# One-level Strassen in both products of the first token pair, with the weight factors made elsewhere

## The chip, the core and the metric

The kernel runs on one core of a Trainium2 chip. That core has five engines with a queue each: TensorE (PE, matrix products; PEld is its weight load), VectorE (DVE), ScalarE (ACT), GpSimd (POOL) and SyncE (SP), which here only issues DMAs. An engine works through its own queue in order, and a semaphore holds it until what an instruction needs is there. The metric is the device time of one launch in microseconds; lower is better. Three runs of the kernel before took 1492.28, 1492.61 and 1493.27 us.

## What is computed

```python
scores = scale * (q_chunk @ k_chunk^T)                 # 8 x 8 heads, 576 tokens in chunks of 64, head size 64
attn   = softmax(scores)
x      = (attn @ v) as [4608 tokens, 512]
p      = domain_probs / sum(domain_probs)              # [4608, 4]
for e in range(4):                                     # w1: [4, 512, 1024], w2: [4, 1024, 512]
    h    = maximum(x @ w1[e], 0)
    out += p[:, e] * (h @ w2[e])
```

Everything is float32. A float32 operand goes to PE as two halves, a high part (a cast to the reduced type `F32R`) and a low part (what is left), and each product is three matmuls: high x high, high x low, low x high.

## The kernel before

**Tiles and stages.** The 4608 tokens are nine sub-blocks of 512. The first one goes alone; the other eight go as four pairs. The 1024 hidden columns of an expert are two halves of 512, so that each sub-block or pair sees eight passes (4 experts x 2 halves); pass n is pass n % 8 of its stage. A pass multiplies x by a 512 x 512 piece of w1, takes the positive part h, and multiplies h by a 512 x 512 piece of w2.

- *First sub-block* (n = 0 in `startup`, n = 1 to 7 in `plain_pass`): both products plain. Four steps for the hidden columns (`plain_hidden`), then four output tiles of 128 tokens (`Tile.whole`), 12 matmuls of 128 x 512 each: 96 in a pass. The attention of pair 0 runs beside them (`Beside`, a generator that is given one step at a time).
- *First pair* (n = 8 to 15, `first_pair_pass`): x w1 by one-level Strassen (`Group`: seven products of 2 x 3 matmuls, in two groups of 128 columns: 84 matmuls), h w2 plain on eight token tiles (96 matmuls). 180 in a pass.
- *Later pairs* (n = 16 to 39): both products by Strassen, 84 + 84 = 168 matmuls in a pass. `first_later_pass` (n = 16) does x w1 alone; each `later_pass` weaves x w1 of its own pass (`g`, `h` steps) with h w2 of the pass before (`a`, `b` steps) in the order `WOVEN`, 28 steps of 6 matmuls; `last_products` does the last h w2 alone.

**Strassen's sums.** The token side needs sums and differences of h (or x) quarters: `Scaled` and `Tokens`. Of each, ACT casts the high part (`hi`) and POOL subtracts it for the low part (`lo`). Names: b11, b22, b12, b21 are quarters, t1 to t4 the sums; each has two halves k. The weight side needs 7 factors per weight and column group: a11, a12, a22 and s1 to s4. `Factors` makes them in the first pair (sums on POOL, casts on ACT, low parts on POOL) and writes them to DRAM in 7 slots per pass and weight; from n = 16 on `ring_load` reads them back, 512 KB a slot, into a ring of three tiles per weight (`wf0` to `wf5`). `ring_next` asks for the slot three further on as soon as a slot's two units are used (`Units.done`).

**What sets the order.** All orders are written out by hand (`tc.manual_schedule()`): a step's matmuls are issued, then the functions listed for that step (`at`), engine by engine in program order. `TILES` says in which pass and step the attention tiles of the next pair come. PE's PSUM results are read by ACT (`keep`) and DVE.

**Lines.** L513 is every product, L326 and L329 the casts and low parts of weights and tokens, L368 the weight sums, L692 and L695 high and low parts of h, L686 sums of h, L680 relu with scaling, L521 relu's low part in the plain product, L814 the plain output, L463 sums of x, L315 the weight loads, L404 and L408 the writes of factors, L418 the ring's loads.

## Time and profile before

| what | value |
|---|---|
| runs | 1492.28, 1492.61, 1493.27 us (median 1492.61) |
| profiled execution, span from first to last instruction | 1490.5 us |
| PE busy | 1482.5 us (99%) |
| DVE, ACT, POOL busy | 945.3, 611.9, 870.6 us (63, 41, 58%) |
| first sub-block, about 0 to 203.5 us | POOL busy 90.7 of the first 203.0 us |
| first pair, about 203.5 to 545.6 us | PE busy 342.10 of 342.10 us, POOL 231.62 |
| later pairs, 545.6 us to the end | POOL busy about 22 of each 38 to 40 us |

The page gives no end-to-end time for the profiled execution beside its span; the median of the runs lies 2.1 us above the span. How to read it: a row "start, length, engine, line, operation, out<-in, xN" merges N instructions in a row of one kind, and a bracket at its end tells how long the engine stood idle before it and who released it. PE's matmuls overlap: a 128 x 512 matmul is listed with 389 ns, but 24 of them in a row take 5.44 us.

### The profile page before, as it was taken

The page shows a single profiled execution, that of the slowest core. Times are in us where ns is not written, and L with a number is a line of the kernel's source. Part 1 is how long each engine was busy: PE and PEld are TensorE (multiplying, and loading weights), DVE is VectorE, ACT ScalarE, POOL GpSimd, SP SyncE. Part 2 cuts the span into 40 slices and gives each one's busy share as a digit, 9 for nine tenths or more (in the row PEclk, how much of TensorE's full clock was granted, in tenths as well). Part 3 has the DMA queues.
Part 4 walks back from the last instruction along what each step waited for, and adds up shares of the span by engine and source line. Part 5 has one row for each costly group of instructions (what it writes and reads, how often), then busy time and mean ns, then how long its engine had stood idle before and what let it go on. Part 6 is the DMA issues. An engine that isn't in the chain of part 4 may idle for free.

```text
span 1490.5 us, 23245 instructions
## 1 busy us (share of the span) xinstructions
PE 1482.5 (99%) x8652; PEld 1219.7 (82%) x8652; DVE 945.3 (63%) x1338; ACT 611.9 (41%) x1143; POOL 870.6 (58%) x666
## 2 busy tenths in 40 slices
PE   8999999999999999999999999999999999999998
PEld 7888888888888888888888888888888888888887
DVE  5454654544444466777776977777778866666666
ACT  3454454444544434434343434343433433333232
POOL 2353587677757616555566755555557655555554
PEclk9999999999999999999999999999999999999999
DMA  6454348977767576767766679667666696666665
GB/s 200 128 158 126 116 156 305 313 244 228 247 228 240 200 265 212 235 196 235 217 213 195 217 209 277 210 217 229 211 196 197 207 244 213 192 206 190 207 196 155
DMA packets 211088, 314.16 MB, mean 211 GB/s; under 512 B 54800, under 2 KB 131360, under 8 KB 210976
## 3 DMA queue, kind: packets, MB, share of 16 engines
q1 hardware_dynamic: 210976, 312.69, 66.5%
q8 instruction: 68, 1.11, 0.3%
q14 instruction: 44, 0.36, 0.1%
HBM read 244.39 MB, written 68.23 MB: 210 GB/s over the span
## 4 chain that ended last, share of the span: by engine, by line
PE 99%; DVE 0%; ACT 0%; issue 0%; ACTq 0%
PE A L513 49%; PE C L513 30%; PE B L513 17%; PE psa L208 1%; PE psa L161 1%; PE B L912 0%; PE C L962 0%; PE A L892 0%; PE B L898 0%; DVE psa L233 0%; DVE e L240 0%; ACT xh L326 0%; PE A L912 0%; PE psa L892 0%; PE C L1433 0%
## 5 line engine op out<-in xcount | busy, mean ns | idle before, releaser
L695 POOL TENSOR_TENSOR hfl<-wraw,hfh 128x512 fp32r<-128x512 f32 x288 | 374.3, 1316 | 215.6 <-ACT hfh L692 213.6
L513 PE MATMUL A<-xh,wf 128*128 128x512 f32 (+1 forms) x1104 | 378.4, 388 | 0.0
L513 PE MATMUL A<-hfh,wf 128*128 128x512 f32 (+1 forms) x768 | 268.4, 391 | 0.0
L692 ACT CAST hfh<-wraw 128x512 fp32r<-128x512 f32 x288 | 176.0, 622 | 214.4 <-DVE wraw L686 63.6
L575 ACT COPY s<-A 128x512 f32<-128x512 f32 x192 | 112.5, 587 | 321.2 <-PE A L513 320.5
L513 PEld LDWEIGHTS A<-xh,wf 128*128 128x128 f32 x1104 | 206.8, 188 | 42.9
L513 PE MATMUL A<-xl,wf 128*128 128x512 f32 (+1 forms) x552 | 213.7, 388 | 0.0
L513 PE MATMUL C<-xh,wf 128*128 128x512 f32 (+1 forms) x600 | 203.3, 388 | 0.7 <-ACT xh L326 0.7
L513 PEld LDWEIGHTS A<-hfh,wf 128*128 128x128 f32 x768 | 144.1, 188 | 31.5 <-DVE acc L742 1.2
L742 DVE TENSOR_TENSOR acc<-A,acc 128x512 f32<-128x512 f32 x174 | 118.7, 683 | 63.3 <-PE A L513 62.7
L513 PE MATMUL A<-hfl,wf 128*128 128x512 f32 x384 | 149.2, 389 | 0.0
L513 PE MATMUL C<-hfh,wf 128*128 128x512 f32 x384 | 133.6, 389 | 0.0
L513 PEld LDWEIGHTS C<-xh,wf 128*128 128x128 f32 x600 | 111.4, 188 | 23.9 <-ACT xh L326 0.8
L329 POOL TENSOR_TENSOR hfl<-wraw,hfh 128x512 fp32r<-128x512 f32 x64 | 85.9, 1371 | 77.0 <-ACT hfh L326 68.9
L513 PE MATMUL B<-xh,wf 128*128 128x512 f32 (+1 forms) x376 | 124.7, 383 | 0.0
L329 POOL TENSOR_TENSOR wf<-wraw,wf 128x512 fp32r<-128x512 f32 x70 | 91.5, 1331 | 55.0 <-ACT wf L326 49.6
L513 PEld LDWEIGHTS A<-xl,wf 128*128 128x128 f32 x552 | 103.5, 188 | 21.1
L513 PE MATMUL C<-xl,wf 128*128 128x512 f32 (+1 forms) x300 | 114.6, 385 | 0.0
L686 POOL TENSOR_TENSOR wf<-wraw,wf 128x512 f32<-128x512 f32 x23 | 29.7, 1292 | 139.3 <-DVE wf L680 139.3
L742 DVE TENSOR_TENSOR acc<-C,acc 128x512 f32<-128x512 f32 x90 | 62.1, 690 | 44.7 <-PE C L513 37.5
L695 POOL TENSOR_TENSOR hfl<-wf,hfh 128x512 fp32r<-128x512 f32 x48 | 70.1, 1461 | 32.4 <-ACT hfh L692 31.9
L513 PEld LDWEIGHTS C<-hfh,wf 128*128 128x128 f32 x384 | 72.1, 188 | 14.9
(185 smaller groups left out, 2747.8 us busy)
## 6 DMA issues: line engine op xcount, KB each, us to landing
wf<-w SPq DMA_DIRECT2D x336, 512.0 KB, 4.1
wraw<-in_w SPq DMA_DIRECT2D x128, 256.0 KB, 3.9
w<-wf SPq DMA_DIRECT2D x112, 256.0 KB, 4.6
qk_in<-in_qk SPq DMA_DIRECT2D x32, 512.0 KB, 4.8
w<-hfl SPq DMA_DIRECT2D x32, 256.0 KB, 3.8
w<-hfh SPq DMA_DIRECT2D x32, 256.0 KB, 3.3
w<-hfh SPq DMA_DIRECT2D x48, 128.0 KB, 2.9
w<-hfl SPq DMA_DIRECT2D x48, 128.0 KB, 2.8
```

The lines of the kernel that those rows point to most:

```text
L161: nc.tensor.matmul(s["sc"][of_half(half), c, slot], lhsT=q, rhs=k, start=True, stop=True)
L208: nc.tensor.matmul(av[of_half(slot % 2), half, head // 2], lhsT=s["v"][of_half(half), head], rhs=s["pt"][of_half(half), c, slot], start=Tr ...
L329: eng.tensor_tensor(out=t[1], in0=src, in1=t[0].bitcast(F32), op=ALU.subtract)
L513: nc.tensor.matmul(out, lhsT=lhs(k, a), rhs=rhs(k, b), start=first and i == 0, stop=last and i == len(parts) - 1, skip_group_check=not (fi ...
L575: nc.scalar.copy(out=t, in_=self.a)
L686: (eng or nc.vector).tensor_tensor(out=self.values[place, k], in0=self.values[a, k], in1=self.values[b, k], op=op)
L692: nc.scalar.copy(out=self.part(name, 0)[:, k], in_=self.values[name, k])
L695: (eng or nc.gpsimd).tensor_tensor(out=self.part(name, 1)[:, k], in0=self.values[name, k], in1=self.part(name, 0)[:, k].bitcast(F32), op=A ...
L742: nc.vector.tensor_tensor(out=acc[key], in0=src, in1=acc[key], op=ALU.add)
```

## The change

1. **First pair.** `first_pair_pass` is gone. The pair runs through `first_later_pass` (now n = 8) and `later_pass` (n = 9 to 39), so h w2 is done by Strassen there too: 168 matmuls a pass for 180.
2. **w2's factors** are made in the first sub-block: sums on DVE (on POOL in pass 0), casts on ACT, low parts on POOL, then 20 writes a pass to the slots (`keep_quad`, `keep`).
3. **w1's factors** for passes 0 to 6 are made in the first pair itself, a column group ("half") at a time: `half_load` fetches it, four sums of 128 x 256 on POOL, and each ring slot, in place of a load, is two casts on ACT and two low parts on POOL of 128 x 256 (`ring_make`, one slot per step at most through `make_next`), and a write for the later pairs. Those of pass 7 are made in passes 2 to 5 (`LAST_W1`, `keep_unit`).
4. **Places.** The x of pair 1 no longer stays in SBUF: each attention tile is written to DRAM (`x_kept`) and read back in pass 15 (`x_back`), as `xraw` now holds the halves. In the first sub-block w1's raw quarters go to accumulator tiles (`acc4` to `acc7`).

```diff
@@ a_copy
+        if pair == 1:
+            tile_x = scratch[0][:, :SUB].rearrange("p (j q) -> p j q", j=NK)
...
+        if pair == 1:
+            nc.sync.dma_start(out=x_kept[:, :, i * P : (i + 1) * P], in_=tile_x)
...
+    def x_back():
+        xraw[1] = xpool.tile([P, NK, PAIR * SUB], F32, name="xraw")
+        for k in range(NK):
+            nc.sync.dma_start(out=xraw[1][:, k], in_=x_kept[:, k])
@@ half factors
+    class HalfFactors:
+        AT = {"a11": 0, "a12": 1, "a21": 2, "a22": 3, "s1": 4, "s2": 5, "s4": 6, "s3": 2}
...
+        def less(self, name, a, b, eng, op=ALU.subtract):
+            (eng or nc.gpsimd).tensor_tensor(
+                out=self.at[name], in0=self.at[a], in1=self.at[b], op=op
+            )
...
+    def ring_make(r):
+        t, (n, k) = ring[0, r], divmod(r, N_SLOT)
+        for u in range(2):
+            g, at = divmod(2 * k + u, 7)
+            src = halves[n_pass + n, g].at[ORDER[0][at]]
+            nc.scalar.copy(out=t[:, u, 0], in_=src)
+            nc.gpsimd.tensor_tensor(out=t[:, u, 1], in0=src, in1=t[:, u, 0].bitcast(F32), op=ALU.subtract)
+        nc.sync.dma_start(out=slots[n, 0, k], in_=t.bitcast(F32))
+
+    def make_next():
+        if making:
+            making.pop(0)()
...
+        if i == 0 and r < n_made:
+            making.append(begin)
+        else:
+            begin()
@@ plain_pass
+        w2 = []
+        add(at, 1, lambda: w2.append(w2_factors(n)), lambda: w2[0].sum1(nc.vector), lambda: w2[0].sum2(nc.vector))
+        add(at, 2, lambda: w2[0].sum3(nc.vector), lambda: w2[0].sum4(nc.vector))
+        for i, quad in enumerate(KEPT):
+            add(at, 2 + i // 2, lambda quad=quad: keep_quad(n, *quad))
+        for i, name in enumerate(("s1", "s2", "s3", "s4")):
+            add(at, (3, 4, 5, 5)[i], lambda name=name: w2[0].make(name))
+            add(at, (4, 5, 6, 6)[i], lambda name=name: w2[0].keep(name))
...
-            add(at, 5, lambda: w_loads(1, n + 1))
+            add(at, 6, lambda: w_loads(1, n + 1, PAIR_QUADS))
...
+        add(at, 0, lambda: half_load(n + 1, 0))
+        add(at, 2, lambda: halves[n + 1, 0].sum1(), lambda: halves[n + 1, 0].sum2())
+        add(at, 3, lambda: halves[n + 1, 0].sum3(), lambda: halves[n + 1, 0].sum4())
+        for r in range(6):
+            add(at, (2, 4, 5, 6, 6, 6)[r], lambda r=r: ring_load(0, r, (RINGS[0] + RINGS[1])[r]))
+            if r < 3:
+                add(at, (2, 4, 5)[r], make_next)
+        add(at, 5, lambda: half_load(n + 1, 1))
+        add(at, 6, *(lambda s=s: getattr(halves[n + 1, 1], s)() for s in ("sum1", "sum2", "sum3", "sum4")))
...
-    def first_pair_pass(n, held, made, beside):
...
@@ first_later_pass
+        add(at, 0, lambda: half_load(n + 1, 0))
+        add(at, 5, lambda: half_load(n + 1, 1))
+        half_sums(at, n + 1, 0, (5, 5, 6, 6))
+        half_sums(at, n + 1, 1, (10, 10, 11, 11))
@@ later_pass
+        if n + 1 < 2 * n_pass - 1:
+            add(at, 5, lambda: half_load(n + 1, 0))
+            add(at, 17, lambda: half_load(n + 1, 1))
+            half_sums(at, n + 1, 0, (9, 10, 11, 13))
+            half_sums(at, n + 1, 1, (23, 25, 26, 27))
+        if n == 2 * n_pass - 1:
+            add(at, 0, x_back)
...
+            make_next()
@@ the main sequence
-        for n in range(n_pass, 2 * n_pass):
-            held, made = first_pair_pass(n, held, made, beside[1])
-        ahead = (None,) * 3
-        for n in range(2 * n_pass, n_run):
-            ahead = (later_pass if n > 2 * n_pass else first_later_pass)(n, *ahead)
+        ahead = first_later_pass(n_pass, held)
+        for n in range(n_pass + 1, n_run):
+            ahead = later_pass(n, *ahead)
```

**Place 1: POOL in the first pass of the woven stage.** Before, this is n = 16: `hfl0` to `hfl5` are low parts of h (hfl0 is b11, hfl2 b22, hfl1 b21, hfl5 t2, hfl4 t1), up to the second half of b21.

```order
L695 TENSOR_TENSOR hfl0_5667<-wraw_5655,hfh0_5665 128x512
L695 TENSOR_TENSOR hfl2_5701<-wraw_5688,hfh2_5699 128x512
L695 TENSOR_TENSOR hfl0_5667<-wraw_5711,hfh0_5665 128x512
L695 TENSOR_TENSOR hfl1_5750<-wraw_5734,hfh1_5748 128x512
L695 TENSOR_TENSOR hfl5_5761<-wraw_5655,hfh5_5759 128x512
L695 TENSOR_TENSOR hfl4_5780<-wraw_5688,hfh4_5778 128x512
L695 TENSOR_TENSOR hfl2_5701<-wraw_5776,hfh2_5699 128x512
L695 TENSOR_TENSOR hfl1_5750<-wraw_5797,hfh1_5748 128x512
```

Now it is n = 8, and the same queue from the fifth ring slot of pass 8 (`wf5`) on reads as follows; `wf` are ring slots being made (two instructions each), `xraw` the half sums.

```order
L489 TENSOR_TENSOR wf5_2724<-xraw_2633,wf5_2724 128x256 x2
L489 TENSOR_TENSOR wf0_2737<-xraw_2633,wf0_2737 128x256 x2
L489 TENSOR_TENSOR wf1_2755<-xraw_2633,wf1_2755 128x256 x2
L786 TENSOR_TENSOR hfl2_2772<-wraw_2753,hfh2_2770 128x512
L444 TENSOR_TENSOR xraw_2633<-xraw_2633 128x256 x4
L786 TENSOR_TENSOR hfl0_2722<-wraw_2786,hfh0_2720 128x512
L489 TENSOR_TENSOR wf4_2813<-xraw_2633,wf4_2813 128x256 x2
L786 TENSOR_TENSOR hfl1_2831<-wraw_2809,hfh1_2829 128x512
L786 TENSOR_TENSOR hfl5_2842<-wraw_2689,hfh5_2840 128x512
```

The eight low parts of h stand in the same order, but ring slots and half sums of the next pass now stand between them.

**Place 2: SP at the end of the first sub-block** (pass 7). Before, where the ring is filled for the first time (end of the first pair), six loads stand in a row:

```order
L418 DMA wf0_5506<-w0_0_0_96 128x1024
L418 DMA wf1_5508<-w0_0_1_97 128x1024
L418 DMA wf4_5510<-w0_0_2_98 128x1024
L418 DMA wf3_5512<-w0_0_3_99 128x1024
L418 DMA wf2_5514<-w0_0_4_100 128x1024
L418 DMA wf5_5516<-w0_0_5_101 128x1024
```

Now the first three slots are made and written (L490), and the load of the second half, `xraw<-in_w1`, stands behind the write of the third, which waits for POOL's low part of that slot:

```order
L490 DMA w0_0_1_98<-wf1_2598 128x1024
L909 DMA out_0<-acc1_521 128x512
L411 DMA w7_1_1_203<-hfl6_2593 128x512
L411 DMA w7_1_4_206<-hfl6_2593 128x512
L490 DMA w0_0_2_99<-wf4_2627 128x1024
L439 DMA xraw_2633<-in_w1 128x4x128 x2
```

**Place 3: DVE in pass 6**, between the low part of the first hidden block (hfl0) and that of the last (the second hfl1). Before:

```order
L521 SCALAR_TENSOR_TENSOR hfl0_1981<-A1_2011,hfh0_1980 128x512
L463 TENSOR_TENSOR xraw_891<-xraw_891 128x2x512
L521 SCALAR_TENSOR_TENSOR hfl1_2039<-B0_2040,hfh1_2038 128x512
L329 TENSOR_TENSOR xl4_2036<-qk_in_2009,xh4_2035 128x1024
L521 SCALAR_TENSOR_TENSOR hfl1_2039<-B1_2059,hfh1_2038 128x512
```

Now, with the four sums of w2 (L389) in the same stretch:

```order
L615 SCALAR_TENSOR_TENSOR hfl0_2233<-A1_2263,hfh0_2232 128x512
L389 TENSOR_TENSOR ws_2286<-wraw_2198,wraw_2194 128x512
L389 TENSOR_TENSOR ws_2286<-ws_2286,wraw_2192 128x512
L557 TENSOR_TENSOR xraw_954<-xraw_954 128x2x512
L615 SCALAR_TENSOR_TENSOR hfl1_2294<-B0_2295,hfh1_2293 128x512
L389 TENSOR_TENSOR wraw_2198<-wraw_2192,wraw_2198 128x512
L389 TENSOR_TENSOR wraw_2196<-wraw_2196,ws_2286 128x512
L346 TENSOR_TENSOR xl4_2291<-qk_in_2261,xh4_2290 128x1024
L615 SCALAR_TENSOR_TENSOR hfl1_2294<-B1_2324,hfh1_2293 128x512
```

Two sums stand ahead of the third block's low part and all four ahead of the fourth's.

More of the change, by code (lines that the diff above doesn't have):

```diff
@@ L310, in w_load @@
     def w_load(i, n, f, k):
-        t = raw[i, f, k] = wpool.tile([P, 2, 2 * P], F32, name="wraw", bufs=N_RAW)
+        if i == 0 and n:
+            t = opool.tile([P, 2, 2 * P], F32, name=f"acc{NK + 2 * f + k}")
+        else:
+            t = wpool.tile([P, 2, 2 * P], F32, name="wraw", bufs=N_RAW)
+        raw[i, f, k] = t
         e, half = divmod(n % n_pass, 2)
```

338 lines of the change are left out of this document (175 added, 163 removed).

## The prediction

> **What bounds the kernel now.** I read the page's busy times and its chain first, then the chain in order of time for the pitch of the matmuls, then busy time by stretches.
>
> ```profile
> span 1490.5 us, 23245 instructions
> ...
> PE 1482.5 (99%) x8652; PEld 1219.7 (82%) x8652; DVE 945.3 (63%) x1338; ACT 611.9 (41%) x1143; POOL 870.6 (58%) x666
> ...
> PE 99%; DVE 0%; ACT 0%; issue 0%; ACTq 0%
> ```
>
> PE is the bound in nearly every moment. The rows below, of the chain in order of time, show how regular it is.
>
> ```profile
> 92.22 5.44 PE A L513 x24
> ...
> 1286.85 4.11 PE A L513 x18
> ...
> 1324.95 4.08 PE A L513 x18
> ...
> 1363.03 4.08 PE A L513 x18
> ```
>
> 24 matmuls in 5.44 us are 0.2267 us each, 6 are a step of 1.36 us. The same point of a pass returns after 1363.03 - 1324.95 = 38.08 us, which is 168 x 0.2267: a later pass without attention has no gap at all. So PE's work is what I save from, and every wait that the change brings to PE is added in full.
>
> ```profile
> 203.50:545.60 342.10, 342.10 (x1971) 281.60 (x1970) 164.93 (x247) 158.45 (x300) 231.62 (x181) 1.00 0.76 256
> 545.60:567.40 21.80, 21.80 (x98) 18.06 (x97) 12.23 (x18) 8.67 (x15) 10.55 (x8) 1.00 0.50 162
> 1324.95:1363.03 38.08, 38.08 (x170) 31.54 (x169) 24.80 (x33) 11.72 (x20) 22.06 (x18) 1.00 0.63 194
> ```
>
> Each row is a stretch: length, then busy time of PE, PEld, DVE, ACT and POOL, clock, DMA. The granted clock is 1.00 throughout. In the first pair (first row) POOL is busy for 231.62 of 342.10 us; in a later pass for 22.06 of 38.08 us.
>
> **What is saved.** In the first pair h w2 goes from 96 to 84 matmuls in each of 8 passes: 96 fewer, all of 128 x 512 on PE's path. 96 x 0.2267 = 21.8 us. Nothing else that PE does there changes in number. DVE, ACT and DMA get the same evacuations and ring traffic as a later pass, which runs without a gap; I cost them at nothing. The same holds for reading x of pair 1 back in pass 15 (up to one or two us if late).
>
> **What POOL gets in the first pair.** The added instructions are 128 x 256, a shape that POOL does not have in this trace, so I bound it by its neighbours.
>
> ```profile
> L368 POOL TENSOR_TENSOR ws<-wraw x16: 1282/1290/1312, 197.7 to 495.9; 128x512 f32<-128x512 f32 x16
> ...
> L463 POOL TENSOR_TENSOR xraw<-xraw x2: 2398/2414/2431, 819.2 to 1135.9; 128x1024 f32<-128x1024 f32 x2
> ...
> L219 ACT COPY xraw<-psa x32: 364/372/374, 59.5 to 1100.0; 128x256 f32<-128x256 f32 x32
> ```
>
> 512 more columns cost 2.41 - 1.29 = 1.12 us, so 256 columns cost 1.29 - 0.56 = 0.73 us; half of 1.29, 0.645, is the lower bound, and 1.29 the upper. I take 0.73. ACT's share of a slot, two casts of about 0.37 us, hides in its idle time (11.72 of 38.08 us busy).
>
> *Term 1, the way from pass 7 into pass 9.* In the pass that begins the woven stage now, POOL has to bring b21's last low part for step a2. Before:
>
> ```profile
> 550.93 1.29 POOL L695 TENSOR_TENSOR hfl<-wraw,hfh 128x512 fp32r<-128x512 f32 x1 [8.84 <-ACT hfh L692]
> ...
> 564.82 2.60 POOL L695 TENSOR_TENSOR hfl<-wraw,hfh 128x512 fp32r<-128x512 f32 x2 [0.26 <-ACT hfh L692]
> ...
> 567.39 2.72 PE B L513 x12
> ```
>
> The last of eight low parts ends at 567.42, a2 starts at 567.39 and needs it with its fifth matmul, 0.91 us on. 0.88 us of room, with 10.55 us of work in 21.8. Now the same stretch on PE is 21.8 + 2.72 us (the output tile held over from pass 7) + 0.91 = 25.4 us. POOL's queue holds eight low parts, 10.55 us, six ring slots, 12 x 0.73 = 8.8, and twelve half sums, 12 x 0.73 = 8.8: 28.1 us, 2.7 more than the stretch has even from a standing start. And it does not start standing. POOL in pass 7:
>
> ```profile
> 185.72 5.44 PE B L513 x24
> ...
> 194.25 3.54 POOL L329 TENSOR_TENSOR hfl<-wraw,hfh 128x512 fp32r<-128x512 f32 x2 [1.01 <-ACT hfh L326]
> ...
> wraw<-in_w SPq DMA_DIRECT2D x128, 256.0 KB, 3.9
> qk_in<-in_qk SPq DMA_DIRECT2D x32, 512.0 KB, 4.8
> ```
>
> w2's low parts end at 197.79, 12.1 us after the pass's first matmul. Then come four half sums and three slots, 10 x 0.73 = 7.3 us, and four low parts of w2's sums, 4 x 1.29 = 5.2: 24.6 us. The load of the second half is queued on SP behind the third slot's write; two loads of the kind above take about 5 us with their issue, so POOL goes on at 29.6 us and is through with the 28.1 us at 57.7. PE's need is at 19.04 (seven steps of 2.72 in pass 7) + 25.4 = 44.4 us. **PE waits 13.3 us**, in pieces at the first h step (slot 3), at a1 and at a2. Bounds: with 0.645 for a small one, w2's low parts at 1.29 each (done at 9.2) and a load of 3.9 us it is 5 us; with POOL's instructions stretched by a tenth and 7 us for the load, 18.
>
> *Term 2, five boundaries between passes 9 and 14.* Each of these passes has 14 low parts for the ring and 8 half sums, 22 x 0.73 = 16.1 us, on top of 22.06: 38.2 us of POOL in a pass of 38.08 plus about 1.2 per attention tile. Before, around a boundary:
>
> ```profile
> 1308.55 3.80 POOL L695 TENSOR_TENSOR hfl<-wraw,hfh 128x512 fp32r<-128x512 f32 x3 [0.16 <-ACT hfh L692]
> 1312.81 1.29 POOL L695 TENSOR_TENSOR hfl<-wraw,hfh 128x512 fp32r<-128x512 f32 x1 [0.47 <-ACT hfh L692]
> ...
> 1316.71 1.29 POOL L695 TENSOR_TENSOR hfl<-wraw,hfh 128x512 fp32r<-128x512 f32 x1 [1.35 <-ACT hfh L692]
> ...
> 1315.43 2.72 PE B L513 x12
> ...
> 1319.51 2.72 PE C L513 x12
> ```
>
> 1312.81 is b21, needed by a2 at 1315.43 + 0.91; 1316.71 is t1, ended at 1318.00 and needed by a5 at 1319.51 + 0.91 = 1320.42: 2.4 us of room. From step 23 on, four half sums and two slots now stand ahead of t1: 8 x 0.73 = 5.8 us. The idle times in the brackets take 2.0, the room 2.4: 1.4 us of wait, at a5. Later low parts have 5 us of room. Five boundaries: 7 us; three have an attention tile in the late steps, which gives PE other work first, so I take **6 us** (0 to 12).
>
> **What the first sub-block gets.** *Term 3.* Four sums of w2 on DVE and four more low parts on POOL in each pass.
>
> ```profile
> 174.84 5.44 PE C L513 x24
> ...
> 175.51 0.69 DVE L521 SCALAR_TENSOR_TENSOR hfl<-B,hfh 128x512 fp32r<-128x512 f32 x1 [0.75 <-ACT hfh L520]
> ...
> 167.90 8.01 POOL L329 TENSOR_TENSOR hfl<-wraw,hfh 128x512 fp32r<-128x512 f32 x4 [7.09 <-ACT hfh L326]
> ...
> 96.67 5.04 POOL L329 TENSOR_TENSOR hfl<-wraw,hfh 128x512 fp32r<-128x512 f32 x4 [8.08 <-DMA wraw<-in_w]
> ...
> L686 DVE TENSOR_TENSOR wraw<-wf,wraw 128x512 f32<-128x512 f32 x48 | 72.4, 1507 | 4.5 <-POOL hfl L695 3.5
> ```
>
> In pass 6 the fourth hidden block's low part ends at 176.20; the first output tile starts at 174.84 and needs it at its twelfth matmul, 177.33: 1.1 us of room, and some 1.0 us of idle DVE ahead of it. Four sums from SBUF cost 0.69 us each when alone and 1.51 beside POOL (last row): 2.8 to 6.0 us, so 0.7 to 3.9 us of wait; POOL's two rows, four low parts in 8.01 us in pass 6 and in 5.04 us in pass 3, show that pass 6 is the crowded kind. I take 2.5. Passes 2 to 5 have attention instead and more idle DVE: 1 us for all. Pass 1 is short of time too:
>
> ```profile
> 44.53 6.59 SPq L315 DMA_DIRECT2D wraw<-in_w  x4
> ...
> 48.19 2.55 POOL L329 TENSOR_TENSOR hfl<-wraw,hfh 128x512 fp32r<-128x512 f32 x2 [6.33 <-ACT hfh L326]
> ...
> 55.13 2.72 PE C L513 x12
> ```
>
> w2's loads were issued from 44.5, split from 48.2 and needed at 55.1. Now they stand behind the writes of w2's factors of pass 0, whose last low part POOL ends at about 41.9 + 4 x 1.3 = 47.1; with 2.5 us of issues and 4 us to landing they are there at 53.6, and two casts and four low parts later it is 57 at least: 1.5 us. **Term 3: 5 us** (1 to 10). Pass 7's own wait is inside term 1, which POOL sets.
>
> The skill has a rule for the crowding: the Trainium skill, "SBUF — State Buffer", section "Who interferes with whom", says that a DVE instruction with two SBUF inputs and a GpSimd instruction that reads SBUF lock each other out for the whole instruction. The 8.01 us against 5.04 agree; by it each of the four sums in a plain pass could wait for a whole POOL instruction, and term 3 would go to its upper end.
>
> **The sum.** -21.8 + 13.3 + 6 + 5 = +2.5 us on the span of 1490.5, so 1493; the median of runs lies 2.1 us above the span: **1495 us**, the saving given back and a little more. A measurement of this kernel can tell about 0.2%, 3 us, from no change.
>
> **Rivals.**
>
> *POOL keeps up, and it is faster: 1480 us.* The terms near their lower bounds (5 + 2 + 2 = 9) leave 12.8 us of gain. It happens if a small POOL instruction costs nearer 0.645 than 0.73 and its idle time before the woven stage is used; it decides at a2 of pass 9. For it: POOL's idle 8.84 us ahead of 550.93; against it: 28.1 us of queue in 25.4. Chance 0.30. The Trainium skill, "GPSIMD Engine Reference", section "3.1 Elementwise — side-by-side cycle accounting", gives about 2.6 cycles an element at 1.2 GHz: 0.555 us for 256 as an estimate without a start-up cost, which would favour this case; no row here has the shape.
>
> *All is hidden: 1471 us* (1492.6 - 21.8). Only if none of the terms exists; the rows at 567 and 1318 speak against it. Chance 0.06.
>
> *The first pair becomes POOL's: 1508 us.* If the added instructions meet DVE's SBUF sums as in pass 6, POOL's 38.2 us a pass become 41 or 42, against 39.6 on PE: some 2 us more in each of five passes, and 2 to 4 more in term 1. For it: 8.01 against 5.04 us; against it: in the later passes POOL's low parts still take 1.29 at most places. Chance 0.18.
>
> **How the numbers follow.** Forecast 0.46, with its own range from 1489 to 1501 (the terms together from 18 to 30). The range for 8 in 10 reaches to the faster rival's centre and to the slow one's: **1479 to 1508**. Faster by over 0.2% (below 1489.6): 0.06 + 0.28 of the faster rival + 0.02 = 0.36. Slower by over 0.2% (above 1495.6): 0.18 + 0.23 of the forecast = 0.41. Same: 0.23.
>
> **What will show it.** PE's matmul count falls by 96, and its busy time by about 22 us. PE's idle time grows from 8 to over 25 us; in the chain POOL appears, with gaps of PE behind `hfl` or `wf` at the first h step of pass 8 and at a1 and a2 of pass 9, 10 us or more together; POOL is busy over 90% of passes 8 to 13; a POOL row of 128 x 256 shows about 0.73 us. Gaps of 1 to 2 us at a5 of each pass from 10 to 14 show term 2; a wait of PE on `hfl` of DVE in pass 6 shows term 3. I am wrong if PE's row stays full there, or if the small POOL instructions take 0.55 us or less; and if PE is idle for 25 us elsewhere, the sum was right by accident.

## The result

| | before | changed |
|---|---|---|
| median, range, runs | 1492.94 us (1492.28 to 1494.79, 4) | 1533.32 us (1532.28 to 1534.47, 4) |
| profiled execution, its span | 1492.61, 1490.5 us | 1533.17, 1531.4 us |

The changed kernel is slower: ratio 1.0271, 95% interval 1.0256 to 1.0285. I had said 1495 us and a range up to 1508; the cost of the waits was 2.5 times what I summed.

The page of the changed kernel, its span, busy times, the row of PE's granted clock, and the chain by engine:

```profile
span 1531.4 us, 23579 instructions
...
PE 1477.7 (96%) x8556; PEld 1207.4 (79%) x8556; DVE 1052.6 (69%) x1455; ACT 630.4 (41%) x1214; POOL 997.1 (65%) x818
...
PEclk9999988999999999999999999999999999999999
...
PE 79%; POOL 8%; DMA 4%; DVE 3%; issue 3%; ACT 2%; SPq 2%; POOLq 0%; ACTq 0%; DVEq 0%
```

The 96 matmuls are gone (8652 to 8556), but PE's busy time fell by 4.8 us and not by 21.8: the matmuls that are left are listed with 17.0 us more (how much of that is a low clock is worked out at the end). PE's idle time went from 8.0 to 53.7 us. The longest sums of PE's waits (us in total, times, longest):

```profile
PE C L607 <- DVE acc L905: 10.4, 1, 10.4
PE C L607 <- DVE hfl L615: 7.1, 3, 4.6
PE B L607 <- POOL hfl L786: 6.8, 3, 5.0
PE C L607 <- POOL hfl L786: 6.8, 5, 1.4
PE A L607 <- DVE hfl L615: 6.6, 4, 2.2
PE C L607 <- ACT hfh L343: 3.3, 1, 3.3
```

The `hfl` of L786 is what I had forecast. The others are DVE's low parts of hidden blocks in the plain passes, and one wait of 10.4 us for the output tile held over from pass 7, which I had not seen.

**Where it went.** In PE's timeline I took the start of the first matmul of each block of the plain passes and of the woven stage, and in the chain the row of 18 matmuls that returns once a pass:

| start of | before | changed | later by |
|---|---|---|---|
| pass 1 | 43.94 | 43.94 | 0 |
| pass 2 | 67.25 | 75.13 | 7.9 |
| pass 3 | 92.06 | 104.43 | 12.4 |
| pass 6 | 163.80 | 180.09 | 16.3 |
| pass 7 | 185.56 | 209.84 | 24.3 |
| woven stage | 204.65 | 234.16 | 29.5 |

Behind that, three such rows of the changed kernel's first pair, and the same three of the second pair before, where the work per pass is the same:

```profile
331.62 4.08 PE A L607 x18
374.00 4.08 PE A L607 x18
416.62 4.08 PE A L607 x18
```

```profile
617.57 4.08 PE A L513 x18
657.05 4.08 PE A L513 x18
697.98 4.08 PE A L513 x18
```

42.38 us against 39.48, and 42.62 against 40.93. Four such passes lose 2.9 + 1.7 + 2.9 + 1.7 = **9.2 us** (169.98 against 160.82); from the fifth row on nothing differs. From the woven start to the row at 331.62 it is 97.46 us. The same stretch without any loss is 74.46: before, the way from the woven start to the second pair's first row is 617.57 - 204.65 = 412.92, less 21.76 saved, and from this the changed kernel's rest (657.48 - 331.62, less 9.16). So it loses **23.0 us**. In sum 29.5 + 23.0 + 9.2 - 21.8 = +39.9; the rest of +40.9, 1 us, comes at the program's end and I have no cause for it. Every experiment below is read by these three losses.

**The three mechanisms in the trace of the changed kernel.** Pass 1, rows of SP, then of ACT, then of PE:

```profile
47.75 1.09 SPq L411 DMA_DIRECT2D w<-hfl  x2
48.88 2.48 SPq L332 DMA_DIRECT2D wraw<-in_w  x4
...
54.43 0.62 ACT L343 CAST hfh<-wraw 128x512 fp32r<-128x512 f32 x1 [6.82 <-DMA wraw<-in_w]
...
56.74 0.59 ACT L614 ACTIVATE hfh<-A 128x512 fp32r<-128x512 f32 x1
...
58.40 0.51 PE L607 MATMUL C<-hfh,hfh 128*128 128x512 f32 x1 [3.26 <-ACT hfh L343]
59.91 0.80 PE L607 MATMUL C<-hfl,hfh 128*128 128x512 f32 x1 [1.01 <-POOL hfl L346]
65.24 0.51 PE L607 MATMUL C<-hfh,hfl 128*128 128x512 f32 x1 [1.28 <-DVE hfl L615]
```

w2's loads stand behind the last factor write on SP, the first lands at 54.4, and ACT, in order, waits 6.82 us with its cast. Behind the cast stands the relu of a hidden block whose product PE has long finished. PE (last rows) waits for w2's cast and low part, 4.27 us together, and then 1.28 us for the low part of a hidden block. Pass 6, rows of DVE:

```profile
189.69 1.67 DVE L389 TENSOR_TENSOR ws<-ws,wraw 128x512 f32<-128x512 f32 x1
191.28 2.31 DVE L557 TENSOR_TENSOR xraw<-xraw 128x1024 f32<-128x1024 f32 x1
...
194.12 1.17 DVE L389 TENSOR_TENSOR wraw<-wraw 128x512 f32<-128x512 f32 x1
195.21 1.75 DVE L389 TENSOR_TENSOR wraw<-wraw,ws 128x512 f32<-128x512 f32 x1
196.88 2.29 DVE L346 TENSOR_TENSOR xl<-qk_in,xh 128x1024 fp32r<-128x1024 f32 x1
199.09 0.68 DVE L615 SCALAR_TENSOR_TENSOR hfl<-B,hfh 128x512 fp32r<-128x512 f32 x1
```

The last hidden block's low part comes behind w2's sums and x's at 199.09; PE waited for it for 4.6 us. Start of the woven stage, rows of SP, POOL and DVE:

```profile
237.92 0.32 SPq L490 DMA_DIRECT2D w<-wf  x1
238.28 1.38 SPq L439 DMA_DIRECT2D xraw<-in_w  x2
...
244.17 1.21 SPq L1302 DMA_DIRECT2D ws<-p_t  x2
...
242.87 2.88 POOL L444 TENSOR_TENSOR xraw<-xraw 128x256 f32<-128x256 f32 x4 [4.98 <-DMA xraw<-in_w]
...
250.14 0.69 DVE L771 SCALAR_TENSOR_TENSOR wraw<-B,ws 128x512 f32<-128x512 f32 x1 [12.30 <-DMA ws<-p_t]
250.75 0.74 DVE L905 SCALAR_TENSOR_TENSOR acc<-C,pr,acc 128x512 f32<-128x512 f32 x1
```

The probabilities of the first pair (`ws`) are issued behind ring slot 2's write, the half load, an output and the factor writes, all paced by POOL. DVE waits 12.30 us for them with the first scaled hidden block, and behind that instruction, in DVE's order, stands the held tile's evacuation, for whose bank PE waits. Four half sums in 2.88 us are 0.72 each.

### The profile page after: what moved, and what is told of

Same layout as the page of the kernel before. It is cut to its first block, busy times and chain, and to the rows that moved or that the text cites. A ratio compares the mean times of both kernels' runs of the same rounds, so it can differ in the third digit from the quotient of the medians.

```text
span 1531.4 us, 23579 instructions
## 1 busy us (share of the span) xinstructions
PE 1477.7 (96%) x8556; PEld 1207.4 (79%) x8556; DVE 1052.6 (69%) x1455; ACT 630.4 (41%) x1214; POOL 997.1 (65%) x818
## 4 chain that ended last, share of the span: by engine, by line
PE 79%; POOL 8%; DMA 4%; DVE 3%; issue 3%; ACT 2%; SPq 2%; POOLq 0%; ACTq 0%; DVEq 0%
PE A L607 43%; PE C L607 23%; PE B L607 10%; POOL hfl L786 2%; POOL wf L489 1%; DMA wraw<-in_w 1%; PE psa L208 1%; POOL xraw L444 1%; POOL hfl L346 1%; PE psa L161 1%; SPq L411 1%; POOL hfh L346 1%; DMA w<-hfh 1%; POOL wf L346 1%; DMA acc<-in_w 1%
## 5 line engine op out<-in xcount | busy, mean ns | idle before, releaser
L786 POOL TENSOR_TENSOR hfl<-wraw,hfh 128x512 fp32r<-128x512 f32 x384 | 500.7, 1319 | 229.9 <-ACT hfh L783 227.2
L607 PE MATMUL A<-hfh,wf 128*128 128x512 f32 (+1 forms) x1024 | 358.2, 391 | 0.6 <-ACT acc L831 0.6
L783 ACT CAST hfh<-wraw 128x512 fp32r<-128x512 f32 x384 | 234.2, 622 | 285.0 <-DVE wraw L777 88.8
L607 PEld LDWEIGHTS A<-hfh,wf 128*128 128x128 f32 x1024 | 192.1, 188 | 42.9 <-DVE acc L833 1.8
L607 PE MATMUL C<-xh,wf 128*128 128x512 f32 (+1 forms) x600 | 205.9, 390 | 11.1 <-DVE acc L905 10.4
L833 DVE TENSOR_TENSOR acc<-A,acc 128x512 f32<-128x512 f32 x232 | 158.0, 681 | 78.5 <-PE A L607 77.6
L607 PE MATMUL A<-hfl,wf 128*128 128x512 f32 x512 | 199.0, 389 | 0.0
L607 PE MATMUL C<-hfh,wf 128*128 128x512 f32 x512 | 178.3, 389 | 0.0
L786 POOL TENSOR_TENSOR hfl<-wf,hfh 128x512 fp32r<-128x512 f32 x64 | 92.8, 1451 | 40.8 <-ACT hfh L783 40.4
L607 PEld LDWEIGHTS C<-hfh,wf 128*128 128x128 f32 x512 | 96.1, 188 | 19.8
L607 PEld LDWEIGHTS A<-hfl,wf 128*128 128x128 f32 x512 | 96.1, 188 | 19.5
L607 PE MATMUL C<-hfl,wf 128*128 128x512 f32 x256 | 100.2, 391 | 6.8 <-POOL hfl L786 6.8
```

The costliest lines, as they stand in the source:

```text
L607: nc.tensor.matmul(out, lhsT=lhs(k, a), rhs=rhs(k, b), start=first and i == 0, stop=last and i == len(parts) - 1, skip_group_check=not (fi ...
L783: nc.scalar.copy(out=self.part(name, 0)[:, k], in_=self.values[name, k])
L786: (eng or nc.gpsimd).tensor_tensor(out=self.part(name, 1)[:, k], in0=self.values[name, k], in1=self.part(name, 0)[:, k].bitcast(F32), op=A ...
L833: nc.vector.tensor_tensor(out=acc[key], in0=src, in1=acc[key], op=ALU.add)
```

## The experiments

All are edits of the changed kernel. "Lost" is in the three stretches above: plain passes 1 to 7, woven start to the first row, four boundaries (changed kernel: 29.5, 23.0, 9.2). The first number is the start of the woven stage less 204.65, so it also holds what pass 1 starts late or early: 0.4 us at most, but 2.1 in c5. All three are those of one execution, which need not be the median one: c8's took 1506.24 us, 2.6 above its median.

**One suspect at a time.**

e1_probs, in pass 7:

```diff
+        at[5].insert(0, lambda: (probs_load(n + 1, 0), probs_load(n + 1, 1)))
...
-        add(at, 6, lambda: first_load(1), lambda: probs_load(n + 1, 0), lambda: probs_load(n + 1, 1))
+        add(at, 6, lambda: first_load(1))
```

> Edit: in pass 7 the two loads of the probabilities of pair 1 (into ws) go to SP's queue at step 5, ahead of the writes of s2, s3, s4 and of ring slot 2, not behind them. Theory Q (SP's in-order queue: a load that the next matmuls need stands behind writes that POOL paces): the load is issued at about 232.6 us instead of 244.17, the wait of 10.4 us behind DVE's held tile goes, and with it the low clock after it: 12 us faster than the changed kernel (10 to 15), about 1521. Rival P (POOL's work is the bound up to a2 anyway): the wait only moves to a2's low parts: at most 3 us faster, 1530 or more.

1531.81 us, 1.0256 (1.0237 to 1.0276): 1.5 us less than the changed kernel. Lost 29.7, 20.7, 9.2. The wait for the held tile fell from 10.4 to 2.1 us, and the gain did not come: theory Q had the wait right and its worth wrong, and the time is the one that rival P gave. POOL in this run:

```profile
246.94 2.89 POOL L444 TENSOR_TENSOR xraw<-xraw 128x256 f32<-128x256 f32 x4 [7.20 <-DMA xraw<-in_w]
```

It stood 7.20 us for the half load, now issued behind the probabilities, and PE's waits moved to ACT's copies (4.6 us) and to a2 (4.2).

e2_loads:

```diff
-            add(at, 6, lambda: w_loads(1, n + 1, PAIR_QUADS))
+            at[4].insert(0, lambda: w_loads(1, n + 1, PAIR_QUADS))
...
+        w_loads(1, 1, PAIR_QUADS)
         for quad in KEPT:
             keep_quad(0, *quad)
         for name in ("s1", "s2", "s3", "s4"):
             w2.keep(name)
-        w_loads(1, 1, PAIR_QUADS)
```

> Edit: in the start and in passes 1 to 6 the four loads of w2 of the next pass go to SP's queue ahead of the writes of s1 to s4 (and in the start ahead of the kept quadrants' writes), not behind them. Theory Q: the 30.2 us that the first sub-block lost come mostly from w2 arriving late, ACT's casts of it waiting and the relu standing behind those: 15 to 20 us faster than the changed kernel, 1513 to 1518. Rival D (DVE's four sums of w2 per pass, slowed beside POOL, delay the low parts of the hidden blocks): the gaps ahead of the output tiles stay: at most 5 us faster, 1528 or more.

1520.73 us, 1.0183 (1.0168 to 1.0198): 12.6 us less, more than the rival allows and less than theory Q asked. Lost 15.2, 24.3, 9.2. Passes 1 to 5 lose 3.4 us and not 16.3 (pass 6 starts at 167.16), so 12.9 us of their loss was the place of w2's loads on SP. Passes 6 and 7 still lose 11.8.

n1 asks for the cause of that. Left out there are w2's sums of passes 1 to 7:

```diff
-        add(at, 1, ..., lambda: w2[0].sum1(nc.vector), lambda: w2[0].sum2(nc.vector))
-        add(at, 2, lambda: w2[0].sum3(nc.vector), lambda: w2[0].sum4(nc.vector))
+        add(at, 1, ..., lambda: w2[0].__dict__.update(s1=w2[0].a21, s2=w2[0].a12))
+        add(at, 2, lambda: w2[0].__dict__.update(s3=w2[0].a21, s4=w2[0].a12))
```

> Left out: the four sums of w2 of passes 1 to 7 (28 DVE instructions; s1 to s4 are made from the quadrants a21, a12, a21, a12 as they are), so the output of the first pair is another one. Otherwise the kernel is the one with w2's loads ahead of the factor writes (1520.7 us, 15 us lost between the passes 1 and 7). Theory D (the sums in DVE's queue, and their meeting with POOL's instructions, are what that run still loses in passes 6 and 7): these two lose under 5 us and not 12, POOL's instructions of 128x512 between 66 and 235 us fall from 1.41 us in the mean (100.4 us for 71) to 1.36 or less: 8 us faster than it (5 to 12), 1513. Rival (POOL's factor parts alone keep passes 6 and 7 back): within 3 us of it.

1511.66 us, 1.0130 (1.0116 to 1.0144): 9.1 us less than e2_loads. Lost 4.4, 26.5, 9.3. Passes 6 and 7 lose 0.5 us (167.71 to 189.47 to 209.04, against 163.80 to 185.56 to 204.65 before): DVE's 28 sums are nearly the whole of their loss. But POOL's 128x512 instructions stay at 1.41 us in the mean (99.9 us for 71), so the sums cost by their place in DVE's queue, not by what they do to POOL.

e3_halves:

```diff
-            add(at, i, lambda name=name: getattr(halves[n, g], name)())
+            add(at, i, lambda name=name: getattr(halves[n, g], name)(nc.vector))
```

> Edit: the half sums of w1 of passes 8 to 14 (8 per pass, 128x256) are DVE's work, not POOL's. Theory P (POOL has too much to do in the first pair): the waits at the boundaries of passes 9 to 13 (9.4 us together) and the 5 to 6.8 us at a2 of the first woven pass go: 12 us faster than the changed kernel (9 to 16), about 1521. Rival: DVE, in order and busy for 15 of 21 us, gets the 3 us more in front of evacuations, and PE waits there instead: within 3 us of the changed kernel.

1527.16 us, 1.0227 (1.0212 to 1.0242): 6.2 us less, half of what theory P expected. Lost 31.2, 20.5, 3.8. One pass of the first pair, in the changed kernel and here (length; busy time of PE, PEld, DVE, ACT, POOL; clock; DMA):

```profile
331.62:374.00 42.38, 40.10 (x233) 32.38 (x233) 27.79 (x40) 19.20 (x42) 38.63 (x40) 1.00 0.66 228
```

```profile
330.80:371.23 40.43, 39.83 (x234) 32.47 (x233) 33.65 (x49) 19.00 (x42) 34.42 (x32) 1.00 0.69 237
```

With 34.42 us of work for POOL in this pass, and not 38.63, 5.4 of the 9.2 us at the boundaries are gone; one wait of 0.6 to 0.7 us for POOL is left at each. The 5 us at a2 went too, but PE waited 12.6 us, and not 10.4, for the held tile.

**The clock.** Behind each long wait the granted clock is low. In the changed kernel a matmul of 128x512 then starts every 0.43 us and not every 0.227 (columns as above):

```profile
245.00:247.50 2.50, 0.00 (x0) 0.00 (x0) 0.00 (x0) 0.31 (x1) 2.50 (x5) 0.50 0.95 273
...
252.50:255.00 2.50, 2.50 (x7) 1.95 (x6) 0.00 (x0) 0.26 (x1) 2.50 (x5) 0.50 0.89 356
```

e4_warm and e_warm60 put unread matmuls there, 46 and 60:

```diff
+            if i == 2:
+                spare, x = bank("A0"), xt[0][0]
+                for _ in range(46):
+                    nc.tensor.matmul(spare, lhsT=x[:, 0, :P], rhs=x[:, 0], start=True, stop=True)
```

> Edit: 46 matmuls whose result nobody reads (46 x 0.2267 = 10.4 us) are put on PE between g6 and g5 of the first woven pass, into a bank that is free, where PE waits 10.4 us for the held tile. Nothing else changes. Theory C (the granted clock falls because PE stood still): the clock stays at 1.00 behind the wait, and the kernel is 3 us faster (2 to 5), about 1530, with more work on PE. Rival: the clock falls for another reason, or comes back as slowly: 0 to 2 us slower.

1532.02 us, 1.0258 (1.0243 to 1.0274): inconclusive. The held tile came later in this run, PE still stood for 2.16 us behind the unread matmuls, and the next ten were slow all the same:

```profile
252.50:255.00 2.50, 1.55 (x4) 1.26 (x5) 0.90 (x2) 1.84 (x5) 1.48 (x2) 0.71 1.08 414
255.00:257.50 2.50, 2.50 (x9) 1.92 (x8) 0.00 (x0) 0.00 (x0) 2.50 (x4) 0.60 0.62 247
```

> Edit: as in the run with 46 unread matmuls between g6 and g5 of the first woven pass, but 60 of them (13.6 us), since with 46 PE still stood for 2.2 us and the next 10 matmuls were slow. Theory C (the granted clock falls because PE stood still): no matmul behind this stretch is slower than 0.25 us, the granted clock is 1.00 from 240 to 270 us; the time itself is within 3 us of the changed kernel, since the unread matmuls may outlast the wait. Rival: the clock falls behind the stretch all the same.

1533.20 us, 1.0278 (1.0260 to 1.0295). Without a gap no matmul at this place is slow:

```profile
250.00:255.00 5.00, 5.00 (x23) 4.13 (x22) 1.35 (x2) 1.85 (x5) 1.90 (x3) 1.00 1.03 328
255.00:260.00 5.00, 5.00 (x24) 4.13 (x22) 1.39 (x2) 2.00 (x5) 3.93 (x6) 1.00 0.83 331
```

So theory C holds for this place: PE's standing still lowers the clock. The time is unchanged, since PE then waits at a2 for POOL as before (4.4 us, lost 29.7, 23.7, 9.2).

**Joining them.** c2 has e1's and e2's edits, and:

```diff
-        add(at, 5, lambda: half_load(n + 1, 1))
+        add(at, 1, lambda: half_load(n + 1, 1))
```

> Edits: the two orders on SP together (w2's loads ahead of the factor writes, the probabilities' loads at step 5 of pass 7), and the load of the second half of w1 of pass 8 at step 1 of pass 7, not behind the write of ring slot 2. Theory Q+P (three loads queued behind POOL-paced writes; the third left POOL idle for 7.2 us in the run with the probabilities moved alone, which is why that run gained 2 us and not 10): POOL starts the second half's sums 7 us earlier, and the way from pass 7 to a2 loses about 6 us and not 21: 1507 (1503 to 1511). Rival (POOL's work alone is too much there, wherever the loads stand): no more than 4 us below the run with w2's loads moved alone, 1517 or more.

1521.56 us, 1.0188 (1.0169 to 1.0206): no gain over e2_loads, lost 16.2, 26.8, 9.3. That is what the rival gave (1517 or more), but not for its reason: my own edit did it. The buffer `xraw` is read by x's low parts until 218 us, and a load that waits in SP's queue holds all behind it (rows of SP, then windows; the last two columns are the DMA engines' busy share and GB/s):

```profile
197.13 1.44 SPq L439 DMA_DIRECT2D acc<-in_w  x2
218.41 1.22 SPq L439 DMA_DIRECT2D xraw<-in_w  x2
```

```profile
205.00:210.00 5.00, 5.00 (x24) 4.14 (x23) 3.67 (x3) 4.16 (x9) 4.00 (x4) 1.00 0.00 0
```

c3 is c2 with DVE's sums at steps 4 and 5 and the loads behind them at 5 and 6:

```diff
-        add(at, 1, ..., lambda: w2[0].sum1(nc.vector), lambda: w2[0].sum2(nc.vector))
-        add(at, 2, lambda: w2[0].sum3(nc.vector), lambda: w2[0].sum4(nc.vector))
+        add(at, 4, lambda: w2[0].sum1(nc.vector), lambda: w2[0].sum2(nc.vector))
+        add(at, 5, lambda: w2[0].sum3(nc.vector), lambda: w2[0].sum4(nc.vector))
```

> Edits: those of the run before it in this list, and DVE's four sums of w2 of passes 1 to 7 at steps 4 and 5 (behind the hidden blocks), not at steps 1 and 2; their parts at steps 4 to 6; the loads of w2 and of the probabilities a step later than there, behind the sums that read those buffers. Theory D (what is left of the loss in passes 6 and 7, 8.2 and 3.9 us, is DVE's sums in front of the low parts of hidden blocks): 8 us faster than the run before it (5 to 11), about 1499. Rival: the parts of the sums come later on POOL and meet the ring's making in pass 7, and the loads of w2 come later: within 3 us of it, or slower.

1518.38 us, 1.0175 (1.0156 to 1.0193). Lost 10.9, 25.1, 9.2: pass 6 loses nothing now (166.03 to 187.79), pass 7 loses 8.6, since the sums' parts meet the ring's making on POOL. Both theories were half right.

c4 is c2 with the half sums of passes 10 to 14 on DVE:

```diff
-            add(at, i, lambda name=name: getattr(halves[n, g], name)())
+            add(at, i, lambda name=name: getattr(halves[n, g], name)(nc.vector if n > n_pass + 1 else nc.gpsimd))
```

> Edits: those of the first run of this list, and the half sums of w1 of passes 10 to 14 are DVE's work (40 of 128x256), not POOL's. Theory P (POOL's 22 small instructions per pass cause the waits at the boundaries): the four longer passes come down from 42.4 and 42.6 us to 40.4 and 41.9, as in the run with all half sums on DVE: 5 us faster than the first run of this list (4 to 7). Rival: DVE's order brings waits in their place: within 2 us of it.

1513.51 us, 1.0144 (1.0128 to 1.0160). Lost 16.9, 20.9, 3.8: the 5.5 us at the boundaries as expected, and 2.5 more than that.

c5 puts the loads of pass 7 where their buffers come free, the sums at 4 and 5 in passes 1 to 6 alone, and all half sums of the woven passes on DVE:

```diff
...
+        add(at, 4, lambda: half_load(n + 1, 1), lambda: probs_load(n + 1, 0), lambda: probs_load(n + 1, 1))
...
```

> Edits: w2's loads ahead of the factor writes; DVE's sums of w2 at steps 4 and 5 in passes 1 to 6 but at 1 and 2, as before, in pass 7; in pass 7 the load of the second half of w1 of pass 8 and the two loads of the probabilities at step 4, behind the last read of the buffer xraw (at step 1 the half load held SP's queue until 218.4 us, with the DMA engines at 0.00 to 0.02 of their time from 205 to 220, and all that stood behind it came late) and ahead of the writes of s2 and of slots 1 and 2; the half sums of passes 8 to 14 on DVE. Theory Q+P+D (all that is lost is queue places on SP and DVE and POOL's small work): pass 6 loses 1 and not 8, the wait for the held tile (8 to 12 us) is under 2, the boundaries lose 4 and not 9: 1496 (1490 to 1502). Rival (POOL's work between pass 7 and a2 is too much wherever the loads stand): POOL is never idle there and PE still waits 8 us or more at a1 and a2: 1505 or more.

1504.15 us, 1.0075 (1.0060 to 1.0090): 29 us less than the changed kernel. Lost 14.0, 14.8, 3.7. The wait for the held tile is 1.0 us. The parts of theory Q+P+D came true (pass 6 loses nothing), but not its time: 1504 is above its 1502 and below the rival's 1505, since pass 7 still loses 8.6 us and the stretch behind it 14.8.

c6 gives the second half's four sums of pass 8 to DVE; c7 places pass 7's sums of w2 at steps 0, 1, 4, 4:

```diff
-        add(at, 6, *(lambda s=s: getattr(halves[n + 1, 1], s)() for s in ("sum1", "sum2", "sum3", "sum4")))
+        add(at, 6, *(lambda s=s: getattr(halves[n + 1, 1], s)(nc.vector) for s in ("sum1", "sum2", "sum3", "sum4")))
```

```diff
-            add(at, ((1, 1, 2, 2) if last_pass else (4, 4, 5, 5))[i], ...)
+            add(at, ((0, 1, 4, 4) if last_pass else (4, 4, 5, 5))[i], ...)
```

> Edits: those of the run before it in this list, and the four sums of the second half of w1 of pass 8 on DVE as well. Theory P (POOL's queue ahead of a2 sets the end): 3 us less work on POOL there: 2 to 3 us faster than the run before it. Rival: DVE waits at these sums for the half's load, in front of the held tile: 0 to 4 us slower.

> Edits: those of the first run of this list, and in pass 7 DVE's sums of w2 at steps 0, 1, 4 and 4, not 1, 1, 2 and 2. Theory D (the gaps of 1.7 and 1.4 us in pass 7 are these sums in front of the low parts of hidden blocks): 3 us faster than the first run of this list (1 to 4). Rival: s3 and s4 come later to POOL and push the ring's work back: within 1 us, or slower.

1503.95 (1.0079, 1.0062 to 1.0096) and 1502.37 us (1.0066, 1.0051 to 1.0081); lost 12.2, 16.5, 3.7 and 12.9, 13.9, 3.6. Neither gain is outside what c5's interval allows.

**The last 10 us: order or work?** c8 is c7 with two more places on SP: the first half load of pass 9 at step 4 of pass 7, and each ring slot's write issued when the next slot is made:

```diff
+        if unwritten:
+            unwritten.pop()()
+        unwritten.append(lambda: nc.sync.dma_start(out=slots[n, 0, k], in_=t.bitcast(F32)))
...
```

> Edits: those of the run with pass 7's sums at steps 0, 1, 4 and 4, and two more places on SP: the load of the first half of w1 of pass 9 moves from the first woven step to step 4 of pass 7, and the write of each ring slot is issued when the next slot is made, so that it no longer holds SP while POOL makes the slot's low parts. Theory Q (what is left between pass 7 and a2, 3.3 us behind ACT's copy and 3.4 us behind a slot's load, is again loads behind POOL-paced writes, and ACT's casts of the half behind the late load): those two waits go, with some clock: 6 us faster than that run (3 to 8), about 1496. Rival (POOL is the bound there): the waits move to POOL's low parts: within 1.5 us of it.

1503.69 us, 1.0074 (1.0059 to 1.0090): no gain, lost 14.0, 17.1, 3.8. Theory Q falls here: the waits it named went, and came back as 2.5 us for the held tile and 5.6 behind DVE's work in bank B.

c9 is c8 with work taken off POOL: three of 14 ring low parts per pass on DVE, and s3 and s4 of passes 1 to 6 made behind the next pass's own low parts:

```diff
-            nc.gpsimd.tensor_tensor(out=t[:, u, 1], in0=src, ...)
+            (nc.vector if r > 15 and k % 2 and not u else nc.gpsimd).tensor_tensor(out=t[:, u, 1], in0=src, ...)
...
+        for name in ("s3", "s4") if tail else ():
+            add(at, 2, lambda name=name, of=tail[0]: of.make(name))
+            add(at, 3, lambda name=name, of=tail[0]: of.keep(name))
...
```

> Edits: those of the run before it in this list; the parts of w2's s3 and s4 of passes 1 to 6 are made at step 2 of the next pass, behind w2's own low parts on POOL, not ahead of them; and of each ring slot with an odd place in its pass one of the two low parts is DVE's work, from slot 16 on (3 of 14 per pass). Theory P+Q: passes 6 and 7 lose 3 us less (PE waited for w2's low parts at the first tile of pass 7), the four longer boundaries 3 us less: 1490 (1486 to 1494), that is the kernel before or a little under it. Rival: DVE, which slows POOL's instructions and is slowed by them where both run, gives the gain back: 1495 or more.

1502.45 us, 1.0075 (1.0062 to 1.0088). Lost 7.9, 19.2, 2.6: 6.1 us gained in the plain passes and 1.2 at the boundaries against c8, and 2.1 lost again between them, where PE now waits 7.1 us for the held tile.

c10 puts the probabilities' load at step 3, behind s1 and s2 made at step 2; c11 is c10 with the two sums t4 of pass 8 on DVE; c12 has c7's places of the loads with c9's and c11's work:

```diff
+        add(at, 3, lambda: probs_load(n + 1, 0), lambda: probs_load(n + 1, 1))
+        add(at, 4, lambda: half_load(n + 1, 1))
+        add(at, 5, lambda: half_load(n + 2, 0))
...
```

```diff
-            (4, lambda: sc.sum("t4", 0, nc.gpsimd)),
+            (4, lambda: sc.sum("t4", 0)),
...
```

> Edits: those of c9, with pass 7 in another order: s1 and s2 of w2 are made at step 2, so that ws comes free sooner, s3 and s4 of pass 6 at step 3; the loads of the probabilities at step 3, of the second half of w1 of pass 8 at step 4, of the first half of pass 9 at step 5, and the writes of s1 to s4 of both passes behind them. In c9 the probabilities were issued at 218.95 us behind four half loads and landed at 225.2, and PE waited 7.1 us for the held tile. Theory Q: this wait and its clock go: 7 us faster than c9 (5 to 9), 1495. Rival P (POOL's queue, 204 to 231 us without a break, is what the woven stage waits for): at most 3 us faster.

> Edits: those of c10, and the two sums t4 of the hidden blocks of pass 8 are DVE's work (0.69 us each, where it is idle), not POOL's. In c9 ACT's cast waits 4.8 us for POOL's sum t4, and ACT's evacuation of bank A behind it keeps PE for 2.6 us. Theory (ACT's order behind POOL): that wait goes: 3 us faster than c10 (2 to 5), 1492, level with the kernel before. Rival (another low part of POOL is late there): within 1 us of c10.

> Edits: those of c7; s3 and s4 of w2 of passes 1 to 6 made behind w2's low parts of the next pass, as in c9; pass 7's s1 and s2 made at step 3 and written behind the loads of the half and of the probabilities; three ring low parts per pass on DVE, as in c9; the two sums t4 of pass 8 on DVE, as in c11. So it has c9's gain in pass 7 without the extra half load that stood before the probabilities there. Theory Q: probabilities land at about 221.5 us, PE waits 5 us for the held tile, 2 at a1: 1495 (1491 to 1499). Rival (work, not order: what is taken from one wait of this stage is found in the next): 1500 to 1503, as the last four.

1503.85 us (1.0076, 1.0062 to 1.0090), lost 8.8, 21.3, 2.6; 1501.32 us (1.0057, 1.0044 to 1.0071), lost 8.5, 18.5, 2.6; 1503.24 us (1.0072, 1.0059 to 1.0086), lost 8.0, 20.6, 2.7. c11's own step did what was expected of it (2.5 us off c10, expected 3; PE's wait of 2.54 us behind ACT's evacuation, at 265.70 in c10, is 0.26 in c11); but the levels of 1495, 1492 and 1495 were not reached by any of the three, and the rival of c12 (what is taken from one wait of this stage is found in the next, 1500 to 1503) is the nearer. The eight orders from c5 to c12, all between 1501 and 1504 us, lose 27 to 31 us between pass 1 and the first row each, and mostly share it out differently. c11 where PE stands (windows, then rows of ACT and PE):

```profile
205.00:210.00 5.00, 3.81 (x16) 2.93 (x17) 4.62 (x5) 3.48 (x6) 5.00 (x3) 1.00 0.28 79
210.00:215.00 5.00, 5.00 (x24) 4.10 (x23) 4.87 (x6) 0.72 (x2) 4.92 (x5) 1.00 0.34 79
215.00:220.00 5.00, 3.77 (x17) 2.77 (x15) 0.00 (x0) 0.00 (x0) 4.43 (x6) 1.00 1.01 347
220.00:225.00 5.00, 0.00 (x0) 0.00 (x0) 0.00 (x0) 1.02 (x2) 0.95 (x1) 0.68 1.05 401
...
223.36 0.62 ACT L343 CAST hfh<-wraw 128x512 fp32r<-128x512 f32 x1 [11.28 <-DMA w<-hfh]
...
226.36 0.80 PE L611 MATMUL A<-xh,wf 128*128 128x512 f32 x1 [7.59 <-ACT s L673]
```

From 220 to 225 us PE and DVE stand idle, ACT and POOL nearly so, and the DMA engines move 401 GB/s, all of their time busy: factor writes, half loads, probabilities and ring writes fall into the same 10 us. The wait for the held tile is gone in c10 and c11, as theory Q expected; PE waits 7.9 and 7.6 us for ACT's copy of bank A in its place. That copy stands on ACT behind a cast of w2's factors, which waits 11.28 us until a factor write out of its buffer has landed. So the burst holds PE through one more in-order queue, and it is itself in part the order's work: SP stood for 5.6 us until 211.94 at the load of the probabilities, whose buffer DVE still read, while the DMA engines were busy for a third of their time and finished factors waited behind that load to be written. Whether another order without this burst would be faster is not shown; no run moved the traffic away from it. No order that I ran beats the kernel before; the best, c11, is 0.57% slower.

## Why the prediction was wrong

- **Term 3 is the step that failed most**: 5 us (1 to 10) for passes 1 to 6, measured 24.3 (and pass 7 loses 5.2 more). Pass 1, charged with 1.5, lost 7.9. I had w2 arriving at 53.6 us, and it came at 54.4; but the sum behind that was wrong: four low parts, at 2.55 us for two, end at 58.7 and not at 57, even without the casts, and PE waited 4.27 us for w2's cast and low part. What I did not name is the work behind the waiting cast: the relu of finished hidden blocks in ACT's queue and, behind it, DVE's sums and low parts (1.28 us more of PE, and then the low clock). And I charged 1 us to passes 2 to 5, though the same order on SP returns in every plain pass: passes 1 to 5 lost 16.3 us, and 3.4 with w2's loads ahead. For pass 6 I took 2.5 us out of 0.7 to 3.9; it lost 8.0, and n1 shows that this is DVE's sums. The ends of that range held each sum at 1.51 us at most; three of the four in pass 6 took 1.17 to 1.75, x's instructions between them up to 2.31, and all stood ahead of one low part.
- **Term 1**, 13.3 us (5 to 18; by the prediction's own rows these bounds come to 6 and 19), measured 5.2 in pass 7 and 23.0 behind it. What I described is there: POOL stood 4.98 us for the half load behind slot 2's write (I had 5.0), and PE 5.0 us at a2. What I left out is the load of the probabilities in the same queue behind the same writes. e1_probs shows that it is not simply added: with it out of the way, POOL's wait for the half grows to 7.20 us and the sum stays. How the 23.0 us divide among the waits stays open: no order that I ran brought them below 13.9 (c7).
- **Term 2**, 6 us (0 to 12) in five boundaries, measured 9.2 in four; the fifth, the first in time, lies in the 23.0 us, with a wait of 1.23. The mechanism and POOL's work were right (38.63 us measured, 38.2 by my sum); the size was too low because every other pass waits twice, 0.93 us ahead of bank B and 1.35 ahead of C, where I had one wait of 1.4.
- **The clock** had no term: I read 1.00 throughout the kernel before and priced each wait at its length alone. PE's busy time should have fallen by 21.8 us and fell by 4.8. Of the 17.0 us between, about 11 are the clock: some 50 matmuls between pass 1 and 290 us that start 0.42 to 0.59 us apart and not 0.227. The rest is mostly the matmul ahead of each of the 20 gaps, whose listed 0.39 us no next one overlaps, and the first one behind it. e_warm60 shows the cause of the low clock at one place.
- **Right were**: 21.8 us saved in matmuls (their count), 0.73 us for a POOL instruction of 128x256 (0.72), and no cost at the later evacuations, the casts of the ring and x read back: from the second pair on the distance between the two kernels stays at 39.9 us (974.21 against 934.29, 1479.07 against 1439.19).
- The sign of the forecast was of little worth, since gain and loss were near to each other; the rival that came closest, a POOL-bound first pair at 1508, named the wrong place: the passes it spoke of lost 9.2 us, and 52.5 were lost ahead of them.

On DVE's sums the rule of the Trainium skill that the prediction quotes ("SBUF — State Buffer", section "Who interferes with whom") pointed the right way, to the upper end of term 3. The trace agrees with it on DVE's side: sums from two SBUF inputs, 0.68 us each where POOL stood idle (pass 2, at 89.38 and 89.98), took up to 1.67 and 1.75 beside POOL in pass 6, while the low part that reads PSUM stayed at 0.68. The 0.69 us that the prediction took for a sum alone is the row of such a low part; it happens to be the same size.

## What to carry to other kernels

When a change moves a load behind writes on an in-order queue, price the load's wait by everything that stands behind its first reader on that reader's engine, and do so for every pass in which the order returns, not for the first. A transfer moved ahead helps only from the moment its buffer is free: earlier it holds the queue (c2, and the probabilities in c11), later it holds the engines. And where saved matmuls are weighed against waits, a wait of several microseconds costs more than its length, because the matmuls behind it run slower (1.6 to 2.9 us more here).

## What the runs showed of the hardware that I had not expected

The granted clock falls behind gaps that are short, and the length of the gap does not settle it. Matmuls of 128x512 started every 0.43 us, nearly twice the usual 0.227, for some 8 to 14 matmuls (1.6 to 2.9 us lost) behind gaps of PE of 4.6, 5.0 and 10.4 us in the changed kernel; in it and its 17 edits every gap above 3.4 us between 44 and 300 us was followed by such matmuls. Shorter ones went both ways. A gap of 2.16 us lowered the clock in e4_warm (at 251.29) and in the changed kernel (at 90.47: 0.65 from 92.5 to 97), and left it at 1.00 in e1_probs (at 89.66). One of 1.88 left it at 1.00 in the changed kernel (at 168.82) and lowered it to 0.66 in e_warm60 (at 169.15). The two of 1.7 and 1.4 us within 3 us in pass 7 lowered it in the changed kernel (at 222.70 and 225.38) and in c4, and left it in six other runs with the same pair. One of 3.35 left it at 1.00 in c7 (at 243.13). What decides between these no run here shows. The Trainium skill, "TensorE: Matmul & The Clock Gate", section "HAM oscillation — how this bites in real kernels", gives the rule that PE should have no idle gap above about 3.4 us. The long gaps here agree with it; a gap of 2.16 us was enough too, so here the figure is no safe distance.
